# Twiddle index scaling moved to ScalarE, and the head of kernel generation rearranged around GpSimd constants and an early sine table

## The chip, the cores and the metric

The kernel runs on one core of one Trainium2 chip. A core has TensorE (PE for matmuls, PEld for its weight loads), VectorE (DVE), ScalarE (ACT), GpSimd (POOL) and SyncE (SP), which issues nearly all transfers here. The metric is the device time of one execution in microseconds; lower is better. Times of a kernel are the median of its runs.

## The reference

Four blocks in a row act on a residual stream x of 2048 x 512 in bf16: a sliding local dilated attention, a long convolution of the S4 kind, and the same two again, with the same weights.

```python
def _A_ref(x, wqkv, wo):               # H = 32 heads of 16, window 8, dilation 2
    ...
    idx = pos[:, None] - off[None, :]  # off = arange(8) * 2
    logits = jnp.einsum("bhsd,bhswd->bhsw", q, kg) * scale
    logits = jnp.where(mask[None, None, :, :], logits, -1e9)
    o = jnp.einsum("bhsw,bhswd->bhsd", _softmax(logits), vg)
    return ... @ wo

def _B_ref(u, A_re, A_im, B_re, B_im, C_re, C_im, log_dt, Dskip):
    dt = jnp.exp(log_dt)[:, None]
    logdA = dt * (A_re + 1j * A_im)
    P = jnp.exp(logdA[:, :, None] * l[None, None, :])      # l = 0..2047
    K = jnp.einsum("dn,dnl,dn->dl", Cc, P, dt * Bc).real
    Yf = rfft(pad(u)) * rfft(pad(K))                       # length 4096
    return irfft(Yf)[:, :, :L] + u * Dskip

x = x + _A_ref(_layernorm(x), A_wqkv, A_wo)
x = x + _B_ref(_layernorm(x), ...)
x = x + _A_ref(_layernorm(x), A_wqkv, A_wo)
x = x + _B_ref(_layernorm(x), ...)
```

## The kernel before

Everything runs in stages, in this order (times from the profiled execution):

- **Kernel generation** (`k_gen`, 0 to 110 us). It builds the convolution kernel K. First its head: `dt` becomes a diagonal matrix `dt_diag` (L1029, from the identity `ident` and a small matmul), TensorE turns the six raw parameter matrices (`turned_by`, L1021) and multiplies A and C by `dt` on the way. From the turned `A_re` and `A_im` come the magnitude (exponential, L1040) and the angle in turns (L1041), reduced to half a turn (L1042 to L1044 with the constant `MAGIC`), and its sine and cosine (L1045, L1046), which give z (L1055, L1056). Then z is squared again and again (`square`, `double`, `differ`), powers go to tables `B_t` and `pow_t`, and DVE multiplies up the tables `A_t` (L1084), which TensorE contracts (L1242). `pow_t` needs a copy of one of its planes by a transfer on the SP queue (`power_copy`, L1081) before L1084 first reads it. In between, the first attention's layer norm, q and k projections and first products are woven in.
- **First attention** (`LayerA.core`, 110 to 190 us). DVE makes the products of q and shifted k (`mult`, L333) and of the weights and shifted v (`pv_mult`, L458); TensorE sums them (L341, L345 for logits, L483 for values) and projects v (L389) and q (L216) through two PSUM banks of one tag, `pq`, which ACT empties (L391, L218). v's odd and even rows are projected in the order `VROWS`; once the last row of each half is there, a pair of transfers (L394, L395) shifts v by one partition, and every third argument of the product for a row reads shifted rows.
- **First convolution** (190 to 250 us), **second attention** (250 to 362 us), **second convolution** (to the end).

Four things set the order. On DVE, ACT, PE and SP the program order is kept as written (`tc.manual_schedule(engines=MAN)`), so an instruction that waits holds all behind it on its engine; GpSimd isn't in `MAN`, and its instructions are placed by the framework. The order within `k_gen` after its head is the string `ORDERK`, and that within the first attention's core the string `CORE0`: each letter is one operation (`v` a v projection with its eviction, `q` a q projection, `m` a product L333, `l` its sum, `x` the maximum L405, `e` the exponential L417, `r` the reciprocal L430 and L431, `n` the normalisation L436, `T` a turn with its eviction L447, `P` a value product L458, `S` its sum, `O` the output projection; digits and other letters are events).

`CORE0` also carries the making of the FFT's twiddle factors g2 (`build_g2`). Event `0` calls `indices` for four quarters: for each quarter two iotas of 128 x 512 on GpSimd (L713) and two GpSimd operations (L714) that multiply the index by `2p+1` (`C["p21"]`, one number per partition) and add 16384 or 32768, so that their low 16 bits are the angle of a sine and of a cosine. Events `2` to `5` are their sines on ACT (L718) and the store to DRAM (L719), some 35 us later.

`build_a_consts` makes the identity and masks: iotas on GpSimd, compares on DVE (L88 to L124), before `k_gen` starts. `build_b_consts`, called in `k_gen` after `dt_diag`, makes iotas on GpSimd, per-partition keys on DVE (L621 to L629), values derived from them on DVE (L633 to L637), and hands back `head` (two ACT operations, L641) and `rest` (offsets on DVE, L647 to L654, called after the sine and cosine).

Of the kernel before, what the change touches and what calls it, by code (L numbers as in the profile page):

```python
# [10 lines left out]
ACT = mybir.ActivationFunctionType  # L11
ALU = mybir.AluOpType
# [8 lines left out]
P = 128  # L21
# [47 lines left out]
vmvvv0lvmvqxleqqmlmvrlqmvvnTlmvvxlmevmlvvrlmvvlnTqPxSePS1qmOlPr4SO2PmqS3OlnP5SP67qmOSOlP8ASOPmPb  # L69
BOSlCSwxdeOPaSaarPODVOPnbSOPd9SEOaaPaSOPGFaaPtOSHbSOt  # L70
# [12 lines left out]
def build_a_consts(tc, nc, cpool, tpool):  # L83
    c = {}
# [3 lines left out]
    nc.vector.tensor_scalar(ident[:], it[:], 0, None, ALU.is_equal)  # L88
# [15 lines left out]
    c["e0"] = rows[:]  # L104
    mv = tpool.tile([1, NA, W], I32, name="iota_mask")
    nc.gpsimd.iota(mv[:], pattern=[[1, NA], [-2, W]], base=0, channel_multiplier=0)
    mrow = cpool.tile([1, NA, W], BF16, name="maskrow")
    nc.vector.tensor_scalar(mrow[:], mv[:], 0, -1e9, ALU.is_lt, ALU.mult)
    c["maskrow"] = mrow
    c["zrow"] = rows[:, 64:128]  # L110
    ind = cpool.tile([P, NDT * H], BF16, name="ind32")
    nc.gpsimd.memset(ind[:], 0.0)
    diag = bass.AP(tensor=ind.tensor, offset=ind[:].offset, ap=[list(ind[:].ap[0]), [H + 8, NDT], [1, 8]])
    nc.vector.tensor_tensor(diag, m1[:].unsqueeze(1).to_broadcast([P, NDT, 8]), m2[:].unsqueeze(1).to_broadcast([P, NDT, 8]), ALU.mult)
    c["ind"] = ind[:].rearrange("p (t h) -> p t h", t=NDT)
    sv = tpool.tile([4, 4, H], I32, name="iota_slot")
    nc.gpsimd.iota(sv[:], pattern=[[-1, 4], [0, H]], base=0, channel_multiplier=1)
    slot = cpool.tile([4, 4, H], BF16, name="slot_sel")
    nc.vector.tensor_scalar(slot[:], sv[:], 0, None, ALU.is_equal)
    c["slot"] = slot[:].rearrange("k a h -> k (a h)")  # L120
    mc = tpool.tile([4, max(NCOL), W], I32, name="iota_slot_mask")
    nc.gpsimd.iota(mc[:], pattern=[[4, max(NCOL)], [-2, W]], base=0, channel_multiplier=1)
    keep = cpool.tile([4, max(NCOL), W], BF16, name="slot_mask")
    nc.vector.tensor_scalar(keep[:], mc[:], 0, -1e9, ALU.is_lt, ALU.mult)  # L124
    c["mask"] = keep
    return c
# [66 lines left out]
class LayerA:  # L193
# [416 lines left out]
def build_b_consts(nc, cpool, tmp, w2_dram):  # L610
    C = {}
    EQ = P // 4
    base = tmp.tile([P, EQ, 16], I32, name="w2_base", tag="w2_base")
# [7 lines left out]
    nc.vector.tensor_scalar(t_i[:, 0:1], pi_i[:], 63, 2, ALU.bitwise_and, ALU.logical_shift_right)  # L621
    nc.vector.tensor_scalar(t_i[:, 1:2], pi_i[:], 6, None, ALU.logical_shift_right)
    nc.vector.tensor_scalar(t_i[:, 2:3], pi_i[:], 3, None, ALU.bitwise_and)
    nc.vector.tensor_scalar(t_i[:, 3:4], pi_i[:], 31, 1, ALU.bitwise_and, ALU.logical_shift_right)
    nc.vector.tensor_scalar(t_i[:, 4:5], pi_i[:], 1, None, ALU.bitwise_and)
    nc.vector.tensor_scalar(t_i[:, 5:6], pi_i[:], 5, 1, ALU.logical_shift_right, ALU.bitwise_and)
    nc.vector.tensor_scalar(t_i[:, 6:7], pi_i[:], 63, 1, ALU.bitwise_and, ALU.logical_shift_left)
    nc.vector.tensor_copy(t_i[:, 7:8], pi_i[:])
    pk = tmp.tile([P, 8], F32, name="pk"); nc.vector.tensor_copy(pk[:], t_i[:])  # L629
# [3 lines left out]
    nc.vector.tensor_tensor(aux[:, 0:1], pk[:, 6:7], rik, ALU.add)  # L633
    nc.vector.tensor_scalar(aux[:, 1:2], pf, 2.0, 1.0, ALU.mult, ALU.add)
    C["p21"] = aux[:, 1:2]
    dmask_m = aux[:, 4:6]
    nc.vector.tensor_scalar(dmask_m, d4i[:], d4m, 2.0 / 4096.0, ALU.is_equal, ALU.mult)  # L637
# [6 lines left out]
    def rest():  # L644
        def off_cols(name, rcol, v00, v10, v01, v11):
            o = tmp.tile([P, 2], F32, name=name)
            nc.vector.tensor_scalar(o[:, 0:1], rcol, float(v10 - v00), float(v00), ALU.mult, ALU.add)  # L647
            nc.vector.tensor_scalar(o[:, 1:2], rcol, float(v11 - v01), float(v01), ALU.mult, ALU.add)
            return o
# [3 lines left out]
        nc.vector.scalar_tensor_tensor(eo[:], ak, 512.0, d4k, ALU.mult, ALU.mult)  # L653
        nc.vector.tensor_tensor(off[:], off[:], eo[:].to_broadcast([P, 2]), ALU.add)  # L654
# [42 lines left out]
    return C, head, rest  # L697
# [6 lines left out]
def build_g2(nc, tmp, p21, g2_dram, room):  # L704

    s8 = 2.0 * math.pi / 65536 * SIN_SHRINK
    own = tmp.tile([P, 2, 8 * P], I32, name="g2_i")
    gi = [own[:, 0], own[:, 1], *(room[:, (2 + h) * 16 * P:(3 + h) * 16 * P].bitcast(I32) for h in range(2))]

    def indices(h):  # L710
        for k, bias in enumerate((16384.0, 32768.0)):
            g = gi[h][:, k * 4 * P:(k + 1) * 4 * P]
            nc.gpsimd.iota(g.rearrange("p (a m) -> p a m", m=P), pattern=[[8, 4], [128, P]], base=32 * h, channel_multiplier=0)  # L713
            nc.gpsimd.tensor_scalar(g, g, p21, bias, ALU.mult, ALU.add)  # L714
# [6 lines left out]
    return indices, sines  # L721
# [258 lines left out]
def k_gen(tc, nc, ident, ins, kd, la, x_v, lnst, zero, b_consts):  # L980
# [3 lines left out]
    with ExitStack() as ctx:  # L984
# [8 lines left out]
        late = {}  # L993
        la.front_open()
# [13 lines left out]
        for name in ("A_re", "A_im", "B_re", "B_im", "C_re", "C_im"):  # L1008
# [6 lines left out]
        nc.gpsimd.memset(Bt[:, 0, :, 0, :], 1.0)  # L1015
        nc.gpsimd.memset(Bt[:, 1, :, 0, :], 0.0)
# [8 lines left out]
        nc.scalar.activation(dtr[:], ldt[:], ACT.Exp)  # L1025
        pdt = pst.tile([P, 4, P], F32, name="pt")
# [4 lines left out]
        C, head, rest = b_consts(sp)  # L1031
# [9 lines left out]
        nc.scalar.mul(nat(turn), p_im, 1.0 / TWO_PI)  # L1041
        nc.vector.tensor_scalar(nat(t1[:]), p_im, 1.0 / TWO_PI, MAGIC, ALU.mult, ALU.add)  # L1042
        nc.vector.scalar_tensor_tensor(turn, t1[:], MAGIC, turn, ALU.subtract, ALU.subtract)
        nc.vector.scalar_tensor_tensor(t2[:], turn, -1.0, turn, ALU.mult, ALU.max)  # L1044
        nc.scalar.activation(sn, turn, ACT.Sin, scale=TURN)  # L1045
# [3 lines left out]
        steps, w2_store = rest()  # L1049
# [303 lines left out]
def kernel(  # L1353
# [27 lines left out]
    with tc.tile_pool(name="ctmp", bufs=1) as tmp:  # L1381
        consts = build_a_consts(tc, nc, cpool, tmp)
# [3 lines left out]
    nc.gpsimd.memset(lnst["mh"][:], -0.5)  # L1386
# [6 lines left out]

    with tc.manual_schedule(engines=MAN):
        C = k_gen(tc, nc, consts["ident"], ins, kd, la, x_v, lnst,
# [37 lines left out]
    with tc.tile_pool(name="ctmp_g2", bufs=1) as g2tmp, tc.manual_schedule(engines=MAN):  # L1433
        gx, gs = build_g2(nc, g2tmp, C["p21"], g2_dram, kp[:].rearrange("p q a r -> p (q a r)"))
# [6 lines left out]
              "8": lambda: k_half_fix(0), "9": lambda: k_half_fix(1)}  # L1441
        ev |= {c: K(i // 4, i % 4) for i, c in enumerate("ABCDEFGH")}
# [108 lines left out]
```

## Time and profile before

| | |
|---|---|
| runs before: median, lowest, highest | 412.89, 412.36, 413.35 us |
| the profiled execution: time, span | 412.14, 410.3 us |
| granted TensorE clock, mean | 0.938 |
| iotas L713 on POOL, 109.8 to 129.6 | 8, mean 0.56 us |
| index scalings L714 on POOL, 111.0 to 136.6 | 8, 0.69 to 4.84 us each, 22.6 in all |
| sines L718 on ACT, 148.6 to 156.8 | 4, with one table load ahead of them |

The span runs from the first to the last instruction of the profile. A row of the order of time gives start, duration, engine, line, operation, output and inputs, shapes, count, and in brackets how long the engine stood idle before it and what ended that. Busy time on POOL is rough: an instruction that stands waiting for access counts as busy.

### The profile page before, as it was taken

What the parts mean: (1) busy time and instruction counts of PE and PEld (TensorE: products, weight loads), DVE (VectorE), ACT (ScalarE), POOL (GpSimd) and SP (SyncE); (2) the same over time, 40 slices, a digit from 0 to 9 for tenths busy, and PEclk for the clock granted to TensorE, in tenths of its full rate; (3) what the DMA queues carried; (4) which work ended last, traced back from release to release, by engine and by line L of the source; (5) the groups of instructions that cost most, each with busy time, mean ns of one, the idle gap of its engine ahead of it and who ended that gap; (6) DMA issues with size and microseconds to landing.
All of it is one profiled execution on the core that took longest, in us unless ns stands there. A gap on an engine that the chain in (4) does not pass through costs nothing.

```text
span 410.3 us, 14708 instructions
## 1 busy us (share of the span) xinstructions
PE 322.0 (78%) x6467; PEld 227.0 (55%) x6513; DVE 384.2 (94%) x498; ACT 326.7 (80%) x562; POOL 46.0 (11%) x52
## 2 busy tenths in 40 slices
PE   2000168899899888789988889999998999897794
PEld 2000026567535555566887778543466677566784
DVE  7999999999999999998899989888988999989993
ACT  5999999897556589898999978874656658889972
POOL 3000400000299300001400000000000020000000
PEclk9555569999999999999999999999999999999998
DMA  7930742113015856583245595830043028504516
GB/s 229 388 113 13 84 82 72 33 41 91 13 39 123 213 169 180 159 339 105 71 164 182 180 307 141 311 127 2 0 116 92 3 71 343 158 3 150 161 30 181
DMA packets 62322, 54.17 MB, mean 132 GB/s; under 512 B 33869, under 2 KB 50738, under 8 KB 60978
## 3 DMA queue, kind: packets, MB, share of 16 engines
q1 hardware_dynamic: 62250, 53.22, 42.8%
q8 instruction: 51, 0.84, 0.9%
q14 instruction: 13, 0.11, 0.1%
q10 hardware_dynamic: 8, 0.00, 0.0%
HBM read 30.15 MB, written 13.24 MB: 106 GB/s over the span
## 4 chain that ended last, share of the span: by engine, by line
PE 35%; ACT 18%; DVE 17%; issue 7%; DMA 3%; SPq 2%; DVEq 0%; ACTq 0%
PE pk L1242 5%; DVE pav L458 5%; PE pq L389 5%; DVE prod L333 4%; ACT a1s L774 4%; PE pp L1180 4%; ACT ub L851 3%; PE pp L273 3%; PE pq L216 3%; PE pq L494 2%; DVE t L835 2%; PE pb L869 2%; PE po L483 2%; PE L L341 2%; DMA v_ext<-v_ext 1%
## 5 line engine op out<-in xcount | busy, mean ns | idle before, releaser
L458 DVE TENSOR_TENSOR pav<-attn,v_ext 128x4096 bf16<-128x4096 bf16 (+1 forms) x34 | 73.1, 2168 | 1.2 <-DMA v_ext<-v_ext 0.8
L333 DVE TENSOR_TENSOR prod<-qT,kT_ext 128x4096 bf16<-128x4096 bf16 x29 | 67.1, 2337 | 1.6 <-ACT qT L218 1.1
L1170 PE MATMUL pt<-ident,x_blk 128*128 128x128 bf16 x64 | 6.3, 241 | 42.6 <-DMA w_dram<-w_q 41.1
L1084 DVE TENSOR_TENSOR A_t<-A_t,pow_t 128x1024 bf16<-128x1024 bf16 (+4 forms) x46 | 38.2, 870 | 0.2
L483 PEld LDWEIGHTS <-pav 64*128 64x128 bf16 x1664 | 26.2, 95 | 15.1 <-DVE pav L458 8.5
L483 PE MATMUL po<-ident,pav 64*128 64x64 bf16 x1664 | 29.0, 190 | 6.6 <-DVE pav L458 3.9
L494 PE MATMUL pq<-wop,oT 128*128 128x512 bf16 x122 | 31.6, 379 | 2.5 <-issue 1.9
L851 ACT CAST ub<-pb 128x1024 bf16<-128x1024 f32 x32 | 32.3, 1091 | 0.1
L391 ACT CAST v_ext<-pq 128x512 bf16<-128x512 f32 x32 | 18.8, 586 | 17.0 <-PE pq L389 16.0
L792 PE MATMUL pb<-a1s,w_sb 128*128 128x64 bf16 x768 | 28.0, 193 | 5.4 <-ACT a1s L774 2.3
L389 PE MATMUL pq<-wv,xnT 128*128 128x512 bf16 x121 | 30.1, 379 | 0.6 <-ACT kgs L1250 0.3
L1180 PE MATMUL pp<-xnT,kT_ext 128*128 128x512 bf16 x87 | 25.0, 405 | 7.0 <-ACT qT L1185 2.9
L1170 PEld LDWEIGHTS <-x_blk 128*128 128x128 bf16 x64 | 4.8, 108 | 45.0 <-ACT x_blk L188 43.6
L792 PEld LDWEIGHTS <-w_sb 128*128 128x128 bf16 x768 | 25.0, 98 | 8.0 <-issue 5.2
L774 DVE CAST a1s<-pb 128x1024 bf16<-128x1024 f32 x21 | 25.0, 1217 | 4.1 <-PE pb L785 4.1
L774 ACT CAST a1s<-pb 128x1024 bf16<-128x1024 f32 x27 | 26.4, 1052 | 2.3 <-PE pb L785 2.2
L1242 PEld LDWEIGHTS <-A_t 128*64 128x64 bf16 (+1 forms) x512 | 21.8, 103 | 4.1 <-issue 0.6
L1242 PE MATMUL pk<-B_t,A_t 128*64 128x84 bf16 (+1 forms) x512 | 23.6, 201 | 0.1
L216 PE MATMUL pq<-xnT,kT_ext 128*128 128x512 bf16 x89 | 22.8, 379 | 0.5 <-issue 0.3
L494 PEld LDWEIGHTS <-oT 128*128 128x128 bf16 x128 | 12.4, 98 | 14.0 <-ACT oT L485 1.1
L485 ACT CAST oT<-po 128x512 bf16<-128x512 f32 x26 | 15.0, 577 | 6.0 <-PE po L483 5.9
L389 PEld LDWEIGHTS <-xnT 128*128 128x128 bf16 x128 | 11.6, 97 | 14.1 <-issue 1.9
(258 smaller groups left out, 871.9 us busy)
## 6 DMA issues: line engine op xcount, KB each, us to landing
w_sb<-w_dram SPq DMA_DIRECT2D x8, 1024.0 KB, 6.7
w_dram<-xnT SPq DMA_DIRECT2D x1, 4096.0 KB
kf_ring<-kf_dram SPq DMA_DIRECT2D x13, 256.0 KB, 4.4
kf_ring<-kf_dram SPq DMA_DIRECT2D x26, 128.0 KB, 3.7
v_ext<-v_ext SPq DMA_DIRECT2D x4, 784.0 KB, 6.3
x_blk<-in_A_x_dram SPq DMA_DIRECT2D x4, 512.0 KB, 3.9
kT_ext<-in_A_wqkv_dram SPq DMA_DIRECT2D x4, 512.0 KB, 9.9
x_sb<-in_A_x_dram SPq DMA_DIRECT2D x4, 512.0 KB, 5.2
```

What stands on the lines that cost most here:

```text
L216: nc.tensor.matmul(pq[:], lhsT=self.wqk[:, dt, ft * P:(ft + 1) * P], rhs=self.xnT[:, dt, q * 512:(q + 1) * 512], start=(dt == 0), stop=(dt ...
L333: nc.vector.tensor_tensor(pr, self.qT[q][:, ft].unsqueeze(1).to_broadcast([P, W, 4, P]), kap, ALU.mult)
L389: nc.tensor.matmul(pp[:], lhsT=xnT[:, dt, a * P:(a + 1) * P], rhs=wv[:, dt, :], start=(dt == 0), stop=(dt == NDT - 1))
L458: nc.vector.tensor_tensor(pv[:, i], attn[:, n % 4].unsqueeze(2).to_broadcast([P, W, DH // parts, H]), vap, ALU.mult)
L483: nc.tensor.matmul(po[:, h, 0, i * nt + ft, :], lhsT=pvf[rows, i, w, ft * P:(ft + 1) * P], rhs=ident[rows, rows], start=(w == 0 and ft + i ...
L494: nc.tensor.matmul(pw[:], lhsT=oT[:, ftp, :], rhs=self.wo[:, ftp, :], start=False, stop=(ftp == NDT - 1))
L774: (self.nc.scalar.copy if eng == "act" else self.nc.vector.tensor_copy)(dst, src)
L792: nc.tensor.matmul(p2[:, j, :], lhsT=self.w2[:, ec * EC + j, :], rhs=a1s[:, ec * EC + j, :], start=True, stop=True)
L851: nc.scalar.copy(ub[:], p2)
L1084: return lambda: nc.vector.tensor_tensor(*args)
L1180: nc.tensor.matmul(pps[kind, b, ft][:], lhsT=la.wqk[:, dt, c:c + P], rhs=la.xnT[:, dt, b * 512:(b + 1) * 512], start=(dt == 0), stop=(dt = ...
L1242: nc.tensor.matmul(o, lhsT=lhs, rhs=Bt[:, ri, c * CH + ql].rearrange("p b g -> p (b g)"), start=(not half and j % 4 == 0 and ri == 0), sto ...
```

## The change

- The eight index scalings L714 leave GpSimd. Only four iotas remain (one for each quarter); ACT makes both scaled copies from each (`turns`, one call for each new letter `I` in `CORE0`, eight of them, between the projections).
- `ident` is made by GpSimd, and so are the other compares of `build_a_consts`. The function is now called inside `k_gen`; its iotas and the rest come as two closures, `iotas` and `rest`, called at chosen places. GpSimd is now under program order in `k_gen` (`MAN_ALL`).
- `build_b_consts` returns its per-partition work as closures: `keys` stays on DVE, `keyed` and the offsets of `rest` go to GpSimd, and all of them are called right after `dt_diag`.
- `A_im` is loaded, turned and evicted ahead of `A_re`; the angle's rounding reads the evicted `turn` in SBUF, not PSUM; the exponential comes after the angle on ACT, and the sine's table is then loaded by an explicit instruction.

```diff
-vmvvv0lvmvqxleqqmlmvrlqmvvnTlmvvxlmevmlvvrlmvvlnTqPxSe...
+vmvvv0lvImvIqxleqqmlmvIrlqmvIvInTlmvIvIxlmevImlvvrlmvvlnTqPxSe...
...
-def build_a_consts(tc, nc, cpool, tpool):
+def build_a_consts(nc, cpool, tpool, c):
...
-    nc.vector.tensor_scalar(ident[:], it[:], 0, None, ALU.is_equal)
+    nc.gpsimd.tensor_scalar(ident[:], it[:], 0, None, ALU.is_equal)
...
+    def iotas():
+        nc.gpsimd.iota(u[:], pattern=[[-16, 8]], base=0, channel_multiplier=1)
...
+        nc.gpsimd.memset(ind[:], 0.0)
+
+    def rest():
+        nc.gpsimd.tensor_scalar(nident[:], it[:], 0, -1.0, ALU.is_equal, ALU.mult)
+        m1 = tpool.tile([P, 8], F32, name="ind_m1")
+        nc.gpsimd.tensor_scalar(m1[:], u[:], 0, None, ALU.is_ge)
...
+    def keys():
+        nc.vector.tensor_scalar(t_i[:, 0:1], pi_i[:], 63, 2, ALU.bitwise_and, ALU.logical_shift_right)
...
+        nc.vector.tensor_copy(pk[:], t_i[:])
+
+    def keyed():
+        nc.gpsimd.tensor_tensor(aux[:, 0:1], pk[:, 6:7], rik, ALU.add)
+        nc.gpsimd.tensor_scalar(aux[:, 1:2], pf, 2.0, 1.0, ALU.mult, ALU.add)
+        nc.gpsimd.tensor_scalar(dmask_m, d4i[:], d4m, 2.0 / 4096.0, ALU.is_equal, ALU.mult)
...
     def indices(h):
-        for k, bias in enumerate((16384.0, 32768.0)):
-            g = gi[h][:, k * 4 * P:(k + 1) * 4 * P]
-            nc.gpsimd.iota(g.rearrange("p (a m) -> p a m", m=P), pattern=[[8, 4], [128, P]], base=32 * h, channel_multiplier=0)
-            nc.gpsimd.tensor_scalar(g, g, p21, bias, ALU.mult, ALU.add)
+        nc.gpsimd.iota(gi[h][:, 0:4 * P].rearrange("p (a m) -> p a m", m=P), pattern=[[8, 4], [128, P]], base=32 * h, channel_multiplier=0)
+
+    def turns(i):
+        h, k = divmod(i, 2)
+        src = gi[h][:, 0:4 * P]
+        nc.scalar.activation(src if k else gi[h][:, 4 * P:8 * P], src, ACT.Identity, scale=p21, bias=16384.0 if k else 32768.0)
...
-        for name in ("A_re", "A_im", "B_re", "B_im", "C_re", "C_im"):
+        for name in ("A_im", "A_re", "B_re", "B_im", "C_re", "C_im"):
...
+        iotas()
+        C, keys, keyed, head, rest = b_consts(sp)
+        la.front_zero()
+        nc.gpsimd.memset(lnst["mh"][:], -0.5)
+        nc.gpsimd.memset(Bt[:, 0, :, 0, :], 1.0)
+        nc.gpsimd.memset(Bt[:, 1, :, 0, :], 0.0)
...
-        C, head, rest = b_consts(sp)
+        keys()
+        keyed()
+        steps, w2_store = rest()
+        a_rest()
...
+        p_im = turned_by("A_im", by_dt)
         p_re = turned_by("A_re", by_dt)
-        p_im = turned_by("A_im", by_dt)
-        nc.scalar.activation(nat(a_re), p_re, ACT.Exp)
         nc.scalar.mul(nat(turn), p_im, 1.0 / TWO_PI)
-        nc.vector.tensor_scalar(nat(t1[:]), p_im, 1.0 / TWO_PI, MAGIC, ALU.mult, ALU.add)
+        nc.vector.tensor_scalar(t1[:], turn, MAGIC, None, ALU.add)
         nc.vector.scalar_tensor_tensor(turn, t1[:], MAGIC, turn, ALU.subtract, ALU.subtract)
         nc.vector.scalar_tensor_tensor(t2[:], turn, -1.0, turn, ALU.mult, ALU.max)
+        nc.scalar.activation(nat(a_re), p_re, ACT.Exp)
+        nc.scalar.preload_act_table_set(SIN)
         nc.scalar.activation(sn, turn, ACT.Sin, scale=TURN)
...
-        steps, w2_store = rest()
...
-    with tc.manual_schedule(engines=MAN):
-        C = k_gen(tc, nc, consts["ident"], ins, kd, la, x_v, lnst,
+    with tc.manual_schedule(engines=MAN_ALL):
+        C = k_gen(tc, nc, lambda sp: build_a_consts(nc, cpool, sp, consts), ins, kd, la, x_v, lnst,
...
+        gi = iter(range(8))
+        ev["I"] = lambda: gt(next(gi))
```

The order of DVE, ACT, PE and SP is otherwise the same, letter for letter, and all transfers are the same but for the exchange of the first two.

More of the change, by code (lines that the diff above doesn't have):

```diff
@@ L30 @@
 EXP_LN = "natural_log_exp_and_others"
+SIN = "trig_and_small"
 MAN = {ET.DVE, ET.Activation, ET.PE, ET.SP}
+MAN_ALL = MAN | {ET.Pool}
 SIN_SHRINK = 1.0 - 4e-7
@@ L68 @@
 CORE0 = """
-vmvvv0lvmvqxleqqmlmvrlqmvvnTlmvvxlmevmlvvrlmvvlnTqPxSePS1qmOlPr4SO2PmqS3OlnP5SP67qmOSOlP8ASOPmPb
-BOSlCSwxdeOPaSaarPODVOPnbSOPd9SEOaaPaSOPGFaaPtOSHbSOt
+vmvvv0lvImvIqxleqqmlmvIrlqmvIvInTlmvIvIxlmevImlvvrlmvvlnTqPxSePS1qmOlPr4SO2PmqS3OlnP5SP67qmOSOlP
+8ASOPmPbBOSlCSwxdeOPaSaarPODVOPnbSOPd9SEOaaPaSOPGFaaPtOSHbSOt
 """
@@ L104, in build_a_consts @@
     c["e0"] = rows[:]
+    c["zrow"] = rows[:, 64:128]
+    u = tpool.tile([P, 8], I32, name="iota_ind")
     mv = tpool.tile([1, NA, W], I32, name="iota_mask")
[L106 to L110, printed above, removed]
-    ind = cpool.tile([P, NDT * H], BF16, name="ind32")
-    nc.gpsimd.memset(ind[:], 0.0)
@@ L113, in build_a_consts @@
[L113 to L126, printed above, removed]
+    sv = tpool.tile([4, 4, H], I32, name="iota_slot")
@@ new lines, in build_a_consts @@
+    mc = tpool.tile([4, max(NCOL), W], I32, name="iota_slot_mask")
+    ind = cpool.tile([P, NDT * H], BF16, name="ind32")
+    def iotas():
+        nc.gpsimd.iota(u[:], pattern=[[-16, 8]], base=0, channel_multiplier=1)
+        nc.gpsimd.iota(mv[:], pattern=[[1, NA], [-2, W]], base=0, channel_multiplier=0)
+        nc.gpsimd.iota(sv[:], pattern=[[-1, 4], [0, H]], base=0, channel_multiplier=1)
+        nc.gpsimd.iota(mc[:], pattern=[[4, max(NCOL)], [-2, W]], base=0, channel_multiplier=1)
+        nc.gpsimd.memset(ind[:], 0.0)
@@ new lines, in rest @@
+    def rest():
+        nc.gpsimd.tensor_scalar(nident[:], it[:], 0, -1.0, ALU.is_equal, ALU.mult)
+        m1 = tpool.tile([P, 8], F32, name="ind_m1")
+        nc.gpsimd.tensor_scalar(m1[:], u[:], 0, None, ALU.is_ge)
+        m2 = tpool.tile([P, 8], F32, name="ind_m2")
+        nc.gpsimd.tensor_scalar(m2[:], u[:], 15, None, ALU.is_le)
+        mrow = cpool.tile([1, NA, W], BF16, name="maskrow")
+        nc.gpsimd.tensor_scalar(mrow[:], mv[:], 0, -1e9, ALU.is_lt, ALU.mult)
+        ind8 = cpool.tile([P, 8], BF16, name="ind8")
+        nc.gpsimd.tensor_tensor(ind8[:], m1[:], m2[:], ALU.mult)
+        diag = bass.AP(tensor=ind.tensor, offset=ind[:].offset, ap=[list(ind[:].ap[0]), [H + 8, NDT], [1, 8]])
+        nc.gpsimd.tensor_tensor(diag, m1[:].unsqueeze(1).to_broadcast([P, NDT, 8]), m2[:].unsqueeze(1).to_broadcast([P, NDT, 8]), ALU.mult)
+        slot = cpool.tile([4, 4, H], BF16, name="slot_sel")
+        nc.gpsimd.tensor_scalar(slot[:], sv[:], 0, None, ALU.is_equal)
+        keep = cpool.tile([4, max(NCOL), W], BF16, name="slot_mask")
+        nc.gpsimd.tensor_scalar(keep[:], mc[:], 0, -1e9, ALU.is_lt, ALU.mult)
+        c["ind8"], c["maskrow"], c["mask"] = ind8, mrow, keep
+        c["ind"] = ind[:].rearrange("p (t h) -> p t h", t=NDT)
+        c["slot"] = slot[:].rearrange("k a h -> k (a h)")
@@ L129, in row_stats @@
+    return iotas, rest
 def row_stats(nc, lnst, x_row, a, eng):
@@ L231, in front_open, with front_zero @@
         self.fp = self.fctx.enter_context(tc.tile_pool(name=f"a{l}_front", bufs=2, side="right"))
+    def front_zero(self):
         self.nc.gpsimd.memset(self.kT[:, :, 0:14, 0:1], 0.0)
@@ L618, in build_b_consts @@
     d4i = iota_f32(nc, tmp, "d4i", 2)
+    base = tmp.tile([P, EQ, 16], I32, name="w2_base", tag="w2_base")
     nc.gpsimd.iota(base[:], pattern=[[16, EQ], [4096, 16]], base=8, channel_multiplier=0)
     t_i = tmp.tile([P, 8], I32, name="pk_t")
[L621 to L629, printed above, removed]
+    pk = tmp.tile([P, 8], F32, name="pk")
     ak, rik, d4k, cm, rim, d4m = (pk[:, j:j + 1] for j in range(6))
@@ L632, in build_b_consts @@
     aux = cpool.tile([P, 8], F32, name="aux")
-    nc.vector.tensor_tensor(aux[:, 0:1], pk[:, 6:7], rik, ALU.add)
-    nc.vector.tensor_scalar(aux[:, 1:2], pf, 2.0, 1.0, ALU.mult, ALU.add)
     C["p21"] = aux[:, 1:2]
     dmask_m = aux[:, 4:6]
-    nc.vector.tensor_scalar(dmask_m, d4i[:], d4m, 2.0 / 4096.0, ALU.is_equal, ALU.mult)
+    def keys():
+        nc.vector.tensor_scalar(t_i[:, 0:1], pi_i[:], 63, 2, ALU.bitwise_and, ALU.logical_shift_right)
+        nc.vector.tensor_scalar(t_i[:, 1:2], pi_i[:], 6, None, ALU.logical_shift_right)
+        nc.vector.tensor_scalar(t_i[:, 2:3], pi_i[:], 3, None, ALU.bitwise_and)
+        nc.vector.tensor_scalar(t_i[:, 3:4], pi_i[:], 31, 1, ALU.bitwise_and, ALU.logical_shift_right)
+        nc.vector.tensor_scalar(t_i[:, 4:5], pi_i[:], 1, None, ALU.bitwise_and)
+        nc.vector.tensor_scalar(t_i[:, 5:6], pi_i[:], 5, 1, ALU.logical_shift_right, ALU.bitwise_and)
+        nc.vector.tensor_scalar(t_i[:, 6:7], pi_i[:], 63, 1, ALU.bitwise_and, ALU.logical_shift_left)
+        nc.vector.tensor_copy(t_i[:, 7:8], pi_i[:])
+        nc.vector.tensor_copy(pk[:], t_i[:])
[3 more added lines that the diff above has]
+        nc.gpsimd.tensor_scalar(dmask_m, d4i[:], d4m, 2.0 / 4096.0, ALU.is_equal, ALU.mult)
     f1t = [tmp.tile([P, P], I32, name=f"f1_t{j}") for j in range(2)]
@@ L646, in off_cols @@
             o = tmp.tile([P, 2], F32, name=name)
-            nc.vector.tensor_scalar(o[:, 0:1], rcol, float(v10 - v00), float(v00), ALU.mult, ALU.add)
-            nc.vector.tensor_scalar(o[:, 1:2], rcol, float(v11 - v01), float(v01), ALU.mult, ALU.add)
+            nc.gpsimd.tensor_scalar(o[:, 0:1], rcol, float(v10 - v00), float(v00), ALU.mult, ALU.add)
+            nc.gpsimd.tensor_scalar(o[:, 1:2], rcol, float(v11 - v01), float(v01), ALU.mult, ALU.add)
             return o
@@ L652, in rest @@
         eo = tmp.tile([P, 1], F32, name="w2_eo")
-        nc.vector.scalar_tensor_tensor(eo[:], ak, 512.0, d4k, ALU.mult, ALU.mult)
-        nc.vector.tensor_tensor(off[:], off[:], eo[:].to_broadcast([P, 2]), ALU.add)
+        nc.gpsimd.tensor_scalar(eo[:], ak, 512.0, None, ALU.mult)
+        nc.gpsimd.tensor_tensor(eo[:], eo[:], d4k, ALU.mult)
+        nc.gpsimd.tensor_tensor(off[:], off[:], eo[:].to_broadcast([P, 2]), ALU.add)
         wps = (("Wp", (4, 12, 0, 8)), ("WpJ", (8, 8, 4, 4)))
@@ L695, in rest @@
         return steps, w2_store
-    return C, head, rest
+    return C, keys, keyed, head, rest
 def low16(ap):
@@ L719, in sines @@
         nc.sync.dma_start(g2_dram[:, :, h * 4:(h + 1) * 4, :], gs.rearrange("p (k a m) -> p k a m", k=2, a=4))
-    return indices, sines
+    return indices, turns, sines
 class FftB:
@@ L977, with k_gen @@
 NROW = 641
-def k_gen(tc, nc, ident, ins, kd, la, x_v, lnst, zero, b_consts):
+def k_gen(tc, nc, a_consts, ins, kd, la, x_v, lnst, zero, b_consts):
     B_L = (0, 1, 2, 3, 4, 5, 6, 7, 256, 258, 260, 262, 512, 516, 768, 772, 1024, 1280, 1536, 1792, 2048)
@@ L993, in k_gen @@
         late = {}
+        iotas, a_rest = a_consts(sp)
+        ident = la.c["ident"]
         la.front_open()
@@ L1380 @@
     nc.vector.memset(zt, 0.0)
-    with tc.tile_pool(name="ctmp", bufs=1) as tmp:
-        consts = build_a_consts(tc, nc, cpool, tmp)
+    consts = {}
     lnst = dict(s1=cpool.tile([P, NA], F32, name="ln_s1"), s2=cpool.tile([P, NA], F32, name="ln_s2"),
@@ L1433 @@
     with tc.tile_pool(name="ctmp_g2", bufs=1) as g2tmp, tc.manual_schedule(engines=MAN):
-        gx, gs = build_g2(nc, g2tmp, C["p21"], g2_dram, kp[:].rearrange("p q a r -> p (q a r)"))
+        gx, gt, gs = build_g2(nc, g2tmp, C["p21"], g2_dram, kp[:].rearrange("p q a r -> p (q a r)"))
         G = lambda f, h: lambda: f(h)
@@ L1461 @@
         la.front_open()
+        la.front_zero()
         ln, agg, pts = {}, {}, {}
```

15 lines of the change are left out of this document (removed).

## The prediction

> **What bounds the kernel now.** I read the page's first part, then the stage table, then the order of time in the two stretches that the change touches, and last the landing times of two transfers.
>
> ```profile
> PE 322.0 (78%) x6467; PEld 227.0 (55%) x6513; DVE 384.2 (94%) x498; ACT 326.7 (80%) x562; POOL 46.0 (11%) x52
> ```
> ```profile
> 0.00:10.00 10.00, 3.04 (x25) 2.65 (x25) 7.48 (x37) 5.27 (x10) 3.88 (x21) 1.00 0.78 224
> ...
> 18.00:26.00 8.00, 0.00 (x0) 0.00 (x0) 7.97 (x14) 8.00 (x15) 0.00 (x0) 0.50 0.76 249
> 26.00:60.00 34.00, 7.76 (x31) 3.72 (x33) 33.88 (x59) 33.01 (x65) 5.12 (x4) 0.52 0.40 58
> 60.00:110.00 50.00, 44.34 (x650) 31.62 (x656) 49.66 (x71) 40.77 (x76) 0.21 (x1) 1.00 0.21 49
> 110.00:138.00 28.00, 27.47 (x297) 14.06 (x299) 27.91 (x16) 15.78 (x28) 26.53 (x16) 1.00 0.40 96
> 138.00:168.00 30.00, 25.09 (x751) 17.52 (x756) 29.66 (x20) 26.34 (x52) 0.18 (x1) 1.00 0.59 170
> ```
> Columns of the table: stretch, then busy time of PE, PEld, DVE, ACT, POOL, then granted clock, DMA share, GB/s. From 18 to 168 us DVE is busy all but about 1 us in 150. So a gain counts only if DVE does less or starts earlier there, and an earlier start counts only if nothing fixed in time waits ahead. In 110 to 138 PE is full as well (27.5 of 28).
>
> ```profile
> 1.50 1.64 DVE L88 TENSOR_SCALAR ident<-iota_id 128x128 bf16<-128x128 int32 x1
> 5.65 0.59 ACT L1041 ACTIVATE ws<-pt 128x512 f32<-128x512 f32 x1
> 6.28 0.69 DVE L1042 TENSOR_SCALAR t<-pt 128x512 f32<-128x512 f32 x1 [0.71 <-ACT ws L1041]
> 7.78 1.28 ACT L1045 ACT_TABLE_LOAD   x1 [1.53 <-DVE ws L1043]
> 9.07 0.63 ACT L1045 ACTIVATE ws<-ws 128x512 f32<-128x512 f32 x1
> 9.74 0.69 DVE L1055 TENSOR_TENSOR sq_z<-sq_z,ws 128x512 f32<-128x512 f32 x1 [0.69 <-ACT ws L1045]
> ```
> The head: the sine's table is loaded only after DVE has made `turn`, and DVE then waits for the sine.
>
> ```profile
> L1081 SPq DMA_DIRECT2D pow_t<-pow_t x1: 655/655/655, 20.8 to 20.8; - x1
> ...
> DMA to landing us min/median/max: 5.1/5.1/5.1
> ```
> ```profile
> 26.35 0.29 DVE L1084 TENSOR_TENSOR A_t<-A_t,pow_t 128x256 bf16<-128x256 bf16 x1
> ```
> The first copy of `pow_t` is issued at 20.82 and lands at 25.92. DVE's first use starts at 26.35 without a wait, so it has 0.4 us to spare. The wait before 25.92 is not the copy's own size (128 KB): the DMA engines are 90% busy from 0 to 24 with inputs and the 4 MB of zeros for `w_dram`, and the copy is behind them.
>
> ```profile
> 117.06 2.27 DVE L333 TENSOR_TENSOR prod<-qT,kT_ext 128x4096 bf16<-128x4096 bf16 x1
> 117.49 7.73 POOL L714 TENSOR_SCALAR g_i<-g_i,aux 128x512 int32<-128x512 int32 x2
> 123.19 0.31 ACT L431 ACTIVATE rs<-ssum 128x128 bf16<-128x128 f32 x1
> 124.67 2.69 DVE L333 TENSOR_TENSOR prod<-qT,kT_ext 128x4096 bf16<-128x4096 bf16 x1
> 137.93 0.90 SPq L395 DMA_DIRECT2D v_ext<-v_ext  x1
> 144.29 2.29 DVE L458 TENSOR_TENSOR pav<-attn,v_ext 128x4096 bf16<-128x4096 bf16 x1
> ```
> The same product takes 2.27 or 2.69 us: 2.69 where an L714 on POOL gets in ahead of it. And the L458 at 144.29 reads rows that L395 shifts; that transfer's time to landing in this stretch is 6.2 us, so it lands at 144.15, 0.1 us before its reader starts.
>
> **The change, part by part.**
>
> *Head, the chain.* `ident` goes from DVE to POOL. POOL's shortest L714 (128x512, 0.69) bounds it from above, an iota of 128x128 (0.23) from below; I take 0.4, ready near 1.7. That saves nothing by itself, since the first matmul also needs `dt_row`, done at 2.94. What counts is that DVE no longer makes eight small constants (3.12 to 3.89) ahead of `dt_diag`: it starts at about 3.3 in place of 3.82. A_im's four matmuls then start at 4.0 (before, A_re's at 4.54). With A_im first, ACT's L1041 runs at 4.62 to 5.21 (before, to 6.24). L1042, L1043 and L1044 at 0.72 apart give `turn` at 6.65. ACT does the exponential at 5.12 to 5.72, then the load to 7.02, and the sine starts there, not at 9.07: 2.04 us earlier. The table load now costs 0.37 us of wait, where it cost 1.37. A_im's transfer is issued first instead, and 128 KB issued at 0.74 has landed by 3.28, when A_re's weights are loaded today.
>
> *Head, what is added to POOL.* After `keys` (DVE, near 4.7) POOL runs 21 small operations at 0.09 (pitch of a small iota) to 0.38 us (a 64x64 two-input one) each: done between 7 and 13. `w_off` is the eighth of them, at 8 at the latest, and ACT wants it near 11.5; `off_Wp` near 18.6. Hidden behind ACT's squarings.
>
> *Where the 2.04 us go.* DVE would reach L1084's first `pow_t` at 24.3, ACT would issue the copy near 18.8, but the transfers ahead of it end when they end. The landing is bounded by 25.92 (as now) and 24.4 (DMA down to a third of its share from 24 on). I take 25.92, the row of this very transfer: DVE starts at 25.97 and keeps 0.38 of 2.04. The other end gives 1.94. The rest becomes a new DVE wait of up to 1.66 us before L1084.
>
> *Core, what is taken from POOL.* Eight L714 and four iotas go. Of the DVE instructions in 111 to 139, five are longer than the free 2.28: 2.61 once and 2.69 four times, in all 0.33 + 4 x 0.41 = 2.0 us. DVE would be done with that much less work. The iotas that stay run beside a 2.28 product at 109.8 and do not lengthen it.
>
> *Core, what ACT gets.* Eight operations 128x512 int32 to int32 with one pointer operand. Nearest rows on both sides: L641 with two pointers at 128x512, 0.86; the same line at 128x128 with one pointer 0.39, to which 384 columns at ACT's own slope (0.59 at 512, 1.02 at 1024: 0.85 ns each) add 0.33. I take 0.71, 0.62 in pitch: 5.0 us against ACT's idle 12.2 in 110 to 138. Laid in one by one: the third stands before the first `r`, so `rs` ends at 124.12, not 123.50. DVE, which is 0.74 early by then, waits for it (0.8) and `ex` starts at 124.16, not 124.07. From there it gains on the four other stretches. Evictions for PE come 0.4 to 0.9 later, each before PE reuses the bank; the tightest is `T`, which ends at 128.46 where PE needs its bank at 128.84. PE keeps its pace, and gains the 0.18 us that it waits for DVE today at 130.78.
>
> *Where the 2.0 us go.* The last `v` eviction (137.22) comes from PE, so L394 and L395 are issued 0.18 earlier and land 0.18 earlier. DVE comes 0.8 to 1.0 early to L458 at 144.29 and waits for them. Of 2.0 us 0.18 stay.
>
> *Sum.* 0.38 + 0.18 = 0.56. The profiled execution is 412.14 (span 410.3 and 1.84 around it), the median of the runs shown 412.89, 0.75 above it. 412.14 - 0.56 = 411.58 for that execution, **412.3** for a median of such runs.
>
> **Rivals.**
>
> *The first copy lands early: 410.8.* For: the sum of bytes ahead of it ends near 24. Against: in this trace one of the pieces is late until 25.9. Then 1.94 + 0.18 = 2.1 off the median. Chance 0.18.
>
> *The shift of v is not a wall: 410.5.* Should the v rows land sooner, the 2.0 us stay: 0.38 + 2.0 = 2.4. For: nothing but one landing time stands against it. Against: 6.2 us for both pairs of shifts. Chance 0.08.
>
> *ACT becomes PE's wait in the core: 414.0, slower.* Place: between the fourth and seventh scaling, where `T`, `e` and the evictions queue behind them. It decides from 0.88 us for one scaling (T then ends at 128.84); at 1.2 us T is 0.65 late beyond its margin and the evictions behind `e` add about as much, 1.5 with what `rs` adds, and PE, L395 and L458 move with it: 412.9 + 1.5 - 0.4 = 414.0. For: PE has no idle time there. Against: both rows of such operations are under 0.88. Chance 0.12.
>
> *POOL holds up DVE in the head: 413 to 417, mostly slower.* `ident` took 1.64 us on DVE where comparable small ones take 0.2 to 0.33: it stood until POOL's run of iotas ended. Now L1042's successor reads SBUF and may stand behind POOL's 21 operations. It decides only past 1.66 + 0.38 us, which the new wait hides; if it stands until they end at 12.7, the sine is 5 us later than today: 412.9 + 5.0 - 0.2 = 417.7 at worst. Against: POOL waits three times within them, and DVE can go then. Chance 0.08. The Trainium skill ("SBUF — State Buffer", Who interferes with whom) states it as an exclusive lock: a DVE instruction with two SBUF inputs against a GpSimd one that reads SBUF, the second one blocked fully. The trace agrees in the core, where L714, which reads, lengthens products by 0.41 and the iotas, which only write, do not. For the head it would speak against moving reading operations to POOL beside L1043 and L1044.
>
> **Chances.** Forecast 0.54, with a range of its own of 411.6 to 413.1. 0.2% (0.83 us) is what a measurement here tells from no change. Of the forecast's 0.54, 0.21 lies below 412.06 and 0.33 within; with the two early cases faster is 0.47; same 0.33 + 0.02 of the POOL case = 0.35; slower 0.12 + 0.06 = 0.18. The range goes from 410.3 (both early cases but for their corner) to 414.0.
>
> **What would show it.** Right: the sine (now L1070) at about 7.0; an idle gap on DVE before the first use of `pow_t`, ended by DMA, near 26; products on DVE at 2.28 throughout; a DVE gap of some 0.8 us before the first `ex`, ended by ACT, and another before the third `pav`, ended by the v transfer. Wrong: no gap near 26 (then the whole 2 us stay); PE waiting on ACT between 126 and 137; DVE gaps before 9 us with POOL busy.

## The result

| | median of runs, us | profiled execution, us |
|---|---|---|
| before, same chip | 412.88 | 412.14 (span 410.3) |
| after | 410.00 (409.47 to 411.69) | 410.00 (span 408.2) |
| ratio | 0.9941, 95% interval 0.9917 to 0.9965 | |

Faster: by the ratio 2.4 us, four times the forecast's 0.6. (The ratio is not the quotient of the two medians, which is 0.9930 and would make it 2.9.) As an absolute time 410.0 lies 0.3 below the range; by the ratio, 0.9941 x 412.89 = 410.5, it is just inside. The head, in the order of time of the changed kernel (POOL, ACT and DVE rows):

```profile
1.20 0.55 POOL L90 TENSOR_SCALAR ident<-iota_id 128x128 bf16<-128x128 int32 x1
...
3.22 0.69 DVE L1050 TENSOR_TENSOR dt_diag<-ident,pt 128x512 bf16<-128x512 bf16 x1 [1.64 <-PE pt L1048]
...
4.58 0.60 ACT L1064 ACTIVATE ws<-pt 128x512 f32<-128x512 f32 x1 [1.25 <-PE pt L1036]
...
5.68 1.28 ACT L1069 ACT_TABLE_LOAD   x1
6.98 0.63 ACT L1070 ACTIVATE ws<-ws 128x512 f32<-128x512 f32 x1
...
7.64 0.69 DVE L1079 TENSOR_TENSOR sq_z<-sq_z,ws 128x512 f32<-128x512 f32 x1 [0.54 <-ACT ws L1070]
```

The sine starts at 6.98, not 9.07, and DVE takes it up 2.10 us earlier (7.64 against 9.74). Then the two walls of the prediction, the places where DVE's progress ends at a transfer that lands at its own time. First the `pow_t` copies issued between 15 and 26 us (the landing is that of the first of the two), and DVE's first use of it:

```profile
L1105 SPq DMA_DIRECT2D pow_t<-pow_t x2: 594/621/648, 18.7 to 21.1; - x2
...
DMA to landing us min/median/max: 5.9/5.9/5.9
```
```profile
24.72 0.30 DVE L1108 TENSOR_TENSOR A_t<-A_t,pow_t 128x256 bf16<-128x256 bf16 x1 [0.38 <-DMA pow_t<-pow_t]
```

Issued at 18.7, the copy lands at 24.6; DVE waits 0.38 and starts 1.63 earlier than before (26.35). Then the core (`ex` is the output of the normalisation L443, `mx` of the maximum, `pav` of the value product):

```profile
119.81 2.29 DVE L340 TENSOR_TENSOR prod<-qT,kT_ext 128x4096 bf16<-128x4096 bf16 x1 [0.21 <-PE L L348]
122.52 0.69 DVE L443 TENSOR_TENSOR ex<-ex,rs 128x1024 bf16<-128x1024 bf16 x1 [0.41 <-ACT rs L438]
...
125.58 1.23 DVE L412 TENSOR_REDUCE mx<-L 128x128 bf16<-128x1024 f32 x1 [0.17 <-PE L L323]
...
136.13 1.22 DVE L412 TENSOR_REDUCE mx<-L 128x128 bf16<-128x1024 f32 x1
...
142.69 2.29 DVE L465 TENSOR_TENSOR pav<-attn,v_ext 128x4096 bf16<-128x4096 bf16 x1 [0.94 <-DMA v_ext<-v_ext]
```

All products take 2.29 now. Waits on PE and ACT take 0.8 us of what that frees; at the second maximum `mx` DVE is still 2.56 ahead of before, where the row is

```profile
138.69 1.21 DVE L405 TENSOR_REDUCE mx<-L 128x128 bf16<-128x1024 f32 x1
```

The shift of v then takes it back to 1.60 (142.69 against 144.29). That 1.60 stays to the second attention, where the same sort of shift is waited for 0.45 and not 0.76 (312.69 against 314.72, 2.03 ahead); the span ends 2.1 shorter.

### The profile page after: what moved, and what is told of

Its sections match the earlier page's. It is cut to its first block, busy times and chain, and to the rows that moved or that the text cites. A ratio compares the mean times of both kernels' runs of the same rounds, so it can differ in the third digit from the quotient of the medians.

```text
span 408.2 us, 14701 instructions
## 1 busy us (share of the span) xinstructions
PE 324.5 (80%) x6467; PEld 228.7 (56%) x6513; DVE 379.4 (93%) x478; ACT 331.2 (81%) x570; POOL 31.2 (8%) x61
## 4 chain that ended last, share of the span: by engine, by line
PE 37%; DVE 16%; ACT 14%; DMA 8%; issue 5%; SPq 4%; DVEq 0%; ACTq 0%
PE pq L396 7%; DVE pav L465 6%; PE pk L1266 5%; PE pp L1204 4%; DMA v_ext<-v_ext 3%; ACT a1s L789 3%; PE pq L221 3%; PE pp L280 3%; SPq L1371 3%; DMA w_sb<-w_dram 2%; DVE t L850 2%; ACT ub L866 2%; PE L L348 2%; PE pb L884 2%; DVE prod L340 2%
## 5 line engine op out<-in xcount | busy, mean ns | idle before, releaser
L340 DVE TENSOR_TENSOR prod<-qT,kT_ext 128x4096 bf16<-128x4096 bf16 x29 | 65.6, 2286 | 1.8 <-ACT qT L223 1.1
L807 PE MATMUL pb<-a1s,w_sb 128*128 128x64 bf16 x768 | 29.3, 196 | 5.1 <-ACT a1s L789 2.3
L807 PEld LDWEIGHTS <-w_sb 128*128 128x128 bf16 x768 | 26.3, 100 | 7.7 <-issue 4.8
```

Of the source, the lines that this page charges most:

```text
L340: nc.vector.tensor_tensor(pr, self.qT[q][:, ft].unsqueeze(1).to_broadcast([P, W, 4, P]), kap, ALU.mult)
L807: nc.tensor.matmul(p2[:, j, :], lhsT=self.w2[:, ec * EC + j, :], rhs=a1s[:, ec * EC + j, :], start=True, stop=True)
```

## The experiments

Each run's ratio is to the kernel before on the same chip, with its 95% interval. The changed kernel has 0.9941. The last two columns are starts on DVE, in us; where a cell is blank, nothing rests on it.

| run | ratio | interval | first pow_t product | third pav |
|---|---|---|---|---|
| head alone | 0.9957 | 0.9942 to 0.9971 | 24.76 | 142.66 |
| core alone | 1.0012 | 0.9996 to 1.0028 | 26.34 | 144.18 |
| zeros later | 1.0117 | 1.0088 to 1.0146 | 24.26 | |
| x off the shift | 0.9989 | 0.9969 to 1.0008 | 25.06 | 144.21 |
| split shift | 0.9964 | 0.9948 to 0.9981 | 24.26 | 142.59 |
| core alone, split | 1.0005 | 0.9987 to 1.0023 | | 145.73 |
| weights later | 0.9953 | 0.9932 to 0.9974 | 24.25 | 142.59 |
| three together | 0.9925 | 0.9902 to 0.9949 | 24.26 | 143.31 |
| no early table load | 0.9965 | 0.9943 to 0.9988 | 25.15 | 143.13 |
| split, x early | 0.9915 | 0.9882 to 0.9947 | 24.70 | 141.64 |
| core alone, split, x early | 0.9969 | 0.9947 to 0.9991 | 26.34 | 143.28 |
| all four together | 0.9903 | 0.9865 to 0.9940 | 24.26 | 141.33 |

**Head alone, and core alone.** The changed kernel with `CORE0` and `build_g2` of before; and the reverse.

```diff
-vmvvv0lvImvIqxleqqmlmvIrlqmvIvInTlmvIvIxlmevImlvvrlmvvlnTqPxSe...
+vmvvv0lvmvqxleqqmlmvrlqmvvnTlmvvxlmevmlvvrlmvvlnTqPxSe...
```

> The changed kernel with the old core: GpSimd scales the indices again, no I in the order. Theory (two walls: the first copy of pow_t at 24.6, the second pair of v shifts at 142.7): the head alone gives all that is left, because what the core gains ends at the v shift. The first pow_t product starts at 24.7 as in the changed kernel, the five products in the core are 2.6 to 2.7 again, the third pav starts at 142.6 to 142.9 with a wait of under 0.3 us before it; time 410.0 to 410.8, within 0.5 us of the changed kernel. Rival (the two parts add up): the head gives 1.6 of the 2.4 to 2.9 us, the third pav starts at 143.6 or later, and the time is 0.8 to 1.3 us above the changed kernel.

> The kernel before with the core part alone (four iotas, ACT scales, eight I). Theory (walls): products at 2.28, DVE about 0.9 us early by the second maximum, then a wait of 0.7 to 1.0 us before the third pav, which starts within 0.2 us of 144.3; time within 0.4 us of before (412.5 to 413.2). Rival (the two parts add up): the third pav starts at 143.5 or earlier and the time falls by 0.8 to 1.3 us.

The order of time of DVE, of the head alone and then of the core alone:

```profile
24.76 0.29 DVE L1106 TENSOR_TENSOR A_t<-A_t,pow_t 128x256 bf16<-128x256 bf16 x1 [0.40 <-DMA pow_t<-pow_t]
...
123.10 2.69 DVE L340 TENSOR_TENSOR prod<-qT,kT_ext 128x4096 bf16<-128x4096 bf16 x1
...
142.66 4.50 DVE L465 TENSOR_TENSOR pav<-attn,v_ext 128x4096 bf16<-128x4096 bf16 x2
```
```profile
124.12 0.69 DVE L436 TENSOR_TENSOR ex<-ex,rs 128x1024 bf16<-128x1024 bf16 x1 [0.41 <-ACT rs L431]
...
144.18 4.49 DVE L458 TENSOR_TENSOR pav<-attn,v_ext 128x4096 bf16<-128x4096 bf16 x2 [0.83 <-DMA v_ext<-v_ext]
```

With the long products back (2.69), the head alone still brings the third pav to 142.66, where the changed kernel has it. The core alone has the short products and starts it at 144.18, 0.11 earlier than before, after a wait of 0.83 for the shift. So in DVE's starts the core part adds nothing to the head: each part runs into the same shift. In time the head alone (0.9957) can't be told apart from the whole change (0.9941), and the core alone (1.0012) is no faster than before.

**Zeros later.** The 4 MB go behind the third copy of `pow_t`.

```diff
         x_load(0)
-        zero()
...
             nc.sync.dma_start(Pw[:, :, k, 0, :], Pw[:, :, k, 1, :])
+            if k == 2:
+                zero()
```

> The changed kernel with the 4 MB of zeros issued behind the third copy of pow_t and not ahead of the first. Theory (the copy stands behind the traffic ahead of it): the first copy, issued at 18.7, takes 2 to 3 us and not 5.9, the wait of 0.38 us before the first pow_t product is gone, it starts at 24.3, and all after it comes 0.4 us earlier, the end too: 409.6, if the zeros land before their scatter at 39 us; if they don't, the queue stands there and the time is up to 3 us worse. Rival (the copy is slow of itself): it still takes 5 to 6 us, the wait stays, no change.

SP's issues, and DVE:

```profile
26.95 0.60 SPq L1419 DMA_DIRECT2D w_dram<-xnT  x1
29.78 1.82 SPq L1104 DMA_DIRECT2D pow_t<-pow_t  x1
```
```profile
40.11 1.22 DVE L1109 TENSOR_TENSOR A_t<-A_t,pow_t 128x2048 bf16<-128x2048 bf16 x1 [6.13 <-DMA pow_t<-pow_t]
```

The first copy now takes 2.2 us, not 5.9, and the first wait is gone. But the fourth copy, issued 2.8 us behind the zeros, lands 10 us later, and DVE stands 6.13 us for it. The expectation named the scatter as the risk and 3 us as its price; it was the next copy, and the time rose to 1.2% above before. That a copy waits for the bytes ahead of it is shown twice. The Trainium skill ("DMA: Bandwidth & Descriptors", Queues, rings and completion order) says that each DMA engine takes descriptors in ring order and signals completion only after all its earlier writes; both rows agree.

**x off the second shift.** Two x loads ahead of the four `wop` loads, two behind the first half of K; `load_wo` comes behind the event for this.

```diff
-        ev = {("v", 0): lambda: x_load((0,)), ("v", 1): lambda: x_load((1, 2, 3)),
+        ev = {("v", 0): lambda: x_load((0, 1)),
...
-              "1": lambda: k_half_load(0),
+              "1": lambda: [k_half_load(0), x_load((2, 3))],
```

> The changed kernel with the loads of x moved off the second v shift: two of them ahead of the four loads of the output weights, two behind the loads of the first half of K, none between. Theory (the shift is late because 512 KB loads share the queues with it): each of its two transfers takes 4 to 5 us and not 6.0 and 6.3, the wait of 0.94 us before the third pav falls to 0 to 0.2, and the time to 409.1 to 409.4. Rival 1 (the shift takes 6 us alone): the wait stays at 0.8 to 1.0 and the time at 410.0. Rival 2 (DVE gains, but another wait before 168 us takes it back): the third pav starts at 141.9, and the first layer norm at 165.5 as in the changed kernel.

All three expectations fell: the third pav started at 144.21 after 1.77 of waiting, 1.5 later than in the changed kernel. Of this 0.7 had come ahead of the shift: DVE reached the place at 142.44, not 141.75 (its wait for the first `pow_t` copy was 0.72, not 0.38), and the shift's second transfer was issued at 136.99, not 136.31. The other 0.8 is the longer wait. The x loads had pushed the issues of `wop` to 132.1 to 134.7 (they began at 127.4), right ahead of the shift: the DMA engines are full in 136 to 137, where their busy share in the changed kernel is 0.15.

**Split shift**, on the changed kernel and on the core part alone.

```diff
+                if a in (8, 9):
+                    b = a - 8
+                    nc.sync.dma_start(v[1:113, b:8:2, :], v[0:112, 16 + b:24:2, :])
+                    nc.sync.dma_start(v[113:128, b:8:2, :], v[112:127, 16 + b:24:2, :])
                 if a >= 14:
                     b = a - 14
-                    nc.sync.dma_start(v[1:113, b:14:2, :], v[0:112, 16 + b:30:2, :])
+                    nc.sync.dma_start(v[1:113, 8 + b:14:2, :], v[0:112, 24 + b:30:2, :])
...
```

> The changed kernel with each v shift in two: its first four rows go when they are there, the last three at the old place, so that 381 and not 889 packets of 1 KB remain for the end. Theory (the shift is paced by its own packets, about 250 in a microsecond, so its size is the wall): the last transfer takes 4 to 5 us and not 6.3, the wait of 0.94 us before the third pav falls under 0.2, it starts 0.8 to 0.9 earlier against the second pav's start than in the changed kernel's trace (4.5 to 4.7 us after it, there 5.43), and the time falls to 409.0 to 409.4 where the changed kernel has 410.0. Rival (landing is set by what else is under way, not by size): the wait stays over 0.7.

> The kernel before with the core part alone and the split shift. Theory (the core part makes DVE about 0.9 us early, and only the shift takes that back): the third pav starts at 143.3 to 143.5, not 144.2, and the time is 0.7 to 1.0 us under before, where the core part alone was equal to it. Rival (the core part gains nothing even without the wall, since ACT and PE give it back later): equal to before within 0.3 us.

Both missed: the wait was 0.96 still, and the core alone got worse:

```profile
145.73 4.49 DVE L462 TENSOR_TENSOR pav<-attn,v_ext 128x4096 bf16<-128x4096 bf16 x2 [2.36 <-PE L L428]
```

The profile names PE here, but the last transfer of the shift, issued at 138.93, took 6.7 us to land, so it ended at 145.6. On the changed kernel the smaller last transfer took 5.9, where the whole had taken 6.3, and was issued 0.24 later. The first part had been queued at 133.3 behind 512 KB of x, issued at 132.6, and on the core alone at 135.7 behind x at 135.0; from 136 to 142 the busy share of the DMA engines was 0.87 or more in both. So size by itself isn't the wall. In the changed kernel, unsplit, nothing stands ahead of the shift: the DMA share is 0.15 in 136 to 137 and 0.94 or more from 137 on. Its 889 KB at the 255 GB/s of 137 to 139 would take 3.5 us by this estimate, to 140.5, yet it lands at 142.6; 1.3 MB is moved from 137 to 142, so part of the other x loads, issued behind it from 137.3 on, moves beside it.

**Weight loads later**: `front_w` behind the first copy. And **three together**: this, the split shift, and the third `I` before its `v`.

```diff
-        la.front_w()
...
+            if k == 0:
+                la.front_w()
```
```diff
-...leqqmlmvIrlq...
+...leqqmlmIvrlq...
```

> The changed kernel with the two 512 KB weight loads issued behind the first copy of pow_t and not ahead of it (5 MB ahead of the copy, not 6). Theory (the copy waits for the traffic ahead of it): the first copy lands before 24.2, the wait of 0.38 before the first pow_t product is gone, and the time falls by 0.3 to 0.5 us to 409.6, if the second copy, issued at 26.2, doesn't come late behind the 1 MB. Rival: the second copy is late, DVE waits 0.5 to 2 us at 28, and the time is 410.0 to 411.5.

> The changed kernel with the split shift, the weight loads behind the first copy, and the third index scaling put ahead of its v eviction, so that the reciprocal isn't behind it. If the walls add: 0.4 at 24, up to 0.4 at 122 before the first ex, 0.9 at 142: 1.3 to 1.7 us under the changed kernel, 408.3 to 408.7. If PE, which is full from 110 to 138, takes the place of the reciprocal: 1.2 to 1.3 and waits of DVE on PE near 120 to 126.

Weights later: the copy takes 2.7 us and DVE starts at 24.25, 0.47 earlier. But of this 0.14 is left at the first product of the core (109.44 against 109.58), and the second v shift, behind a PE that is busy for all of 110 to 138, is issued at 135.56, where the changed kernel has 135.62: the third pav gains 0.10. No gain in time is shown. With the three together the first `ex` no longer waits for `rs`, and PE takes 0.67 at the next maximum in its place. The profiled execution took 410.67 where the median is 408.41, with 2.05 us of waiting for the shift; so its trace doesn't show what the median gained.

**Without the early table load.**

```diff
-        nc.scalar.preload_act_table_set(SIN)
```

> The changed kernel without the explicit load of the sine's table. Theory (the early load is worth what the angle takes on DVE beyond the exponential): the load stands behind the angle as before, 6.4 to 7.7, the sine starts at 7.7 and not 6.98, DVE reaches the first pow_t product 0.7 us later, at 25.0, mostly without a wait for the copy; time 0.2 to 0.5 us above the changed kernel (410.0 to 410.5). Rival (the early load is the whole gain of the head): the sine at 9, the time at before's.

```profile
6.44 1.28 ACT L1069 ACT_TABLE_LOAD   x1 [0.78 <-DVE ws L1066]
7.74 0.63 ACT L1069 ACTIVATE ws<-ws 128x512 f32<-128x512 f32 x1
```

ACT's order of time: the load stands behind the angle again and the sine is 0.76 later. So of the 2.1 us in the head the early load is 0.76 and the rearranged chain ahead of it 1.3. In time the two can't be told apart (0.9965 and 0.9941, intervals overlap).

**Split, with x early.** The first 512 KB of x go from ACT at event `0` (issued at 113.1 and not at 132.7), with the split shift kept.

```diff
-        ev = {("v", 0): lambda: x_load((0,)), ("v", 1): lambda: x_load((1, 2, 3)),
+        ev = {("v", 1): lambda: x_load((1, 2, 3)),
...
-              "0": lambda: [gx(h) for h in range(4)],
+              "0": lambda: [nc.scalar.dma_start(x_sb[:, 0:4, :], x_v[:, 0:4, :]), [gx(h) for h in range(4)]],
```

> The changed kernel with the split shift and the first 512 KB of x issued from ACT at the start of the core (near 114 us, where the DMA engines are nearly idle) and not ahead of the second shift. Theory (the split shift failed because x stood ahead of its first part, so that the queue was full from 130 to 140): the first part now starts moving at 133 to 134.5, the last one ends by 141.5, the wait before the third pav is under 0.3 us and the time 409.2 to 409.6. Rival (the last part lands at 142.5 whatever stands ahead): the wait is 0.8 to 1.0 again.

> The kernel before with the core part, the split shift and the first 512 KB of x issued from ACT at the start of the core. Theory (DVE is 0.8 to 0.9 us early and only the shift takes that back): third pav at 143.3 to 143.5, time 0.6 to 1.0 us under before. Rival (the core part gains nothing): equal to before within 0.3 us.

> The changed kernel with all four: weight loads behind the first copy of pow_t, third scaling ahead of its v eviction, split shift, first x load from ACT at the start of the core. If each wall goes: third pav at 141.2 to 141.5 (138.98 + 2.2 in the version without the early x load, which waited until 143.31), and 0.8 to 1.5 us under that version: 407.0 to 407.7. If the shift still lands past 142.5: 408.4, as that version.

The last shift transfer and DVE, changed kernel with both edits:

```profile
L406 SPq DMA_DIRECT2D v_ext<-v_ext x1: 880/880/880, 136.3 to 136.3; - x1
...
DMA to landing us min/median/max: 3.1/3.1/3.1
```
```profile
139.44 2.29 DVE L340 TENSOR_TENSOR prod<-qT,kT_ext 128x4096 bf16<-128x4096 bf16 x1
141.64 4.49 DVE L469 TENSOR_TENSOR pav<-attn,v_ext 128x4096 bf16<-128x4096 bf16 x2
```

And the core part alone with both:

```profile
141.07 2.29 DVE L333 TENSOR_TENSOR prod<-qT,kT_ext 128x4096 bf16<-128x4096 bf16 x1
143.28 4.49 DVE L462 TENSOR_TENSOR pav<-attn,v_ext 128x4096 bf16<-128x4096 bf16 x2
```

The transfer lands in 3.1 us where it took 6.3, and the third pav follows the product without a wait in both. Now the core part shows in time: 1.0012 without the two edits, 0.9969 with them, 1.0 us faster than before (410.55 against 411.52), as expected, and the intervals are apart. On the changed kernel the time, 408.39, is below the 409.2 expected, and with all four the third pav (141.33) is where it was expected. What the two edits give without the core part wasn't tried, but before waits for nothing at that place. Nor was x early without the split, or x early on SP's queue; so whether the earlier time or the other queue mends the shift is open. All four together has the lowest median tried: 407.79, 3.7 us under the 411.52 of before; its interval overlaps that of the changed kernel and of the split with x early.

## Why the prediction came out as it did

- **The head's chain was right**: `dt_diag` 3.22 (forecast 3.3), L1064 at 4.58 (4.62), sine at 6.98 (7.0). `turn` was ready at 6.36, not 6.65, since the first of its three operations reads SBUF in 0.43 where PSUM took 0.69.
- **The step that failed** in the sum is "I take 25.92, the row of this very transfer". The copy landed at 24.6, so the wait was 0.38, not up to 1.66, and the term 0.38 measured 1.63. The landing isn't fixed: with the same traffic ahead, issue plus landing time gives 25.9 in before, 23.9 and 25.3 in two runs with its head, and 24.1, 24.6 and 24.9 in the split, changed and x-off kernels. I took one draw, the latest of all, for the place of the wall; the other end, 1.94 by 24.4, was far nearer, and two of the draws lie even below that bound. The mechanism stood: a DMA wait before this product, and none where fewer bytes were ahead. The rival "the first copy lands early" (410.8) is close to the case that came, and the range holds 410.5 only because it took in the early cases: the sum itself forecast a quarter of the gain.
- **POOL's string** in the head ended at 14.4, not 13, and hid as forecast: the angle's operations keep 0.69 beside it, so that rival fell.
- **The core's sum was right in kind**: products at 2.29, scalings 0.73 to 0.77 (forecast 0.71), 0.41 before the first `ex` with 0.21 on PE ahead of it (0.8 in one wait), 0.94 at the third pav (0.8 to 1.0). Its term 0.18 was too large: L395 was to be issued that much earlier, and on the core alone it was issued at 137.91, 0.02 earlier, for a third pav 0.11 earlier; behind the new head the core part moved that by nothing (142.69 with it, 142.66 without). Each scaling stayed under the 0.88 from which, by the prediction, ACT would have held PE up; the trace of 126 to 137 shows no wait of PE for ACT.
- **The rival "the shift of v is not a wall"** fell in this kernel. Once the shift was mended the core part and that mending came to 1.0 us over before, half of the 2.0 us that the rival gave it; waits of 0.8 us on PE and ACT account for most of the other half.
- Of the last 0.5 of the span's 2.1, 0.3 is the shorter wait for the shift of the second attention (0.45 and not 0.76). With the head alone that wait is 1.07, and yet its span is 408.1, so the place by itself doesn't set the end; where the last half microsecond comes from stays open.

## What to carry to other kernels

Where a transfer ends a wait behind a full queue, its landing in one profile is one draw: bound it by the bytes ahead and the issue time, or look at several executions, before taking it for the place of a wall. A gain that ends at a transfer isn't lost for good; find what the DMA engines move ahead of that transfer and beside it. Here a smaller transfer alone didn't help, and neither did moving x ahead of `wop`; a smaller transfer with x out of its way did. And when a change has several parts, follow each from one wall to the next before adding them up.

## What was not expected of the hardware

- One 128 KB copy with the same 6.8 MB issued ahead of it (six parameters, two blocks of x, zeros, weights) landed 3.1 to 6.2 us after its issue, between 23.9 and 25.9. Without the 1 MB of weights it took 2.7 and 2.8 (two kernels), without the 4 MB of zeros 2.2.
- In the head it is POOL that stands (waits within its instruction), not DVE. The order of time of POOL and of DVE in the changed kernel:

```profile
6.38 0.19 POOL L660 TENSOR_SCALAR w_off<-pk 128x1 f32<-128x1 f32 x1
6.53 0.67 POOL L665 TENSOR_SCALAR w_eo<-pk 128x1 f32<-128x1 f32 x1
...
7.32 0.19 POOL L666 TENSOR_TENSOR w_eo<-w_eo,pk 128x1 f32<-128x1 f32 x1
```
```profile
6.40 0.70 DVE L1067 SCALAR_TENSOR_TENSOR t<-ws 128x512 f32<-128x512 f32 x1
```

A one-column operation takes 0.19, also when DVE starts just behind it (L660), but L665 takes 0.67: it starts while DVE runs L1067 of 0.70, and ends 0.1 after it (7.20 and 7.10). DVE's operation keeps its 0.70. The Trainium skill ("SBUF — State Buffer", Who interferes with whom) says that the pair of ports that the two share is an exclusive lock, and that the order of issue decides which of them is blocked. These rows agree. The prediction looked only at the other direction.
